# A routed expert kernel: the order of its 256-row and 384-row arms, and the place of one activation split at a phase's end

## The chip, the cores and the metric

The kernel runs on one core of one Trainium2 chip. The metric is the device time of one execution in microseconds (us). The kernel before took 606.57 us in the median of three runs (602.05 to 607.6).

## The reference

Two steps follow each other. A packed attention turns q, k, v and p into an activation x of 4608 rows by 512 columns; then each row goes through one of eight experts, the one that a small gate picks for it.

```python
def sm_attn(qq, kk, vv):
    a = softmax(scale * qq @ kk.T)
    return a @ vv
p_packed = sm_attn(p, k, v)                 # 8 x 8 heads, 576 rows, 32 packed rows
x = sm_attn(q, p_packed, p_packed)          # -> 4608 x 512
logits = x @ w_gate + modality_bias[modality_id]
e_idx = argmax(logits)                      # one of 8 experts for each row
for e in range(8):                          # w1: 512 x 1024, w2: 1024 x 512
    rows = e_idx == e
    out[rows] = gate_w[rows] * (relu(x[rows] @ w1[e]) @ w2[e])
```

## The kernel before

The attention fills about the first half of the time. The second half works through **slots**. A slot is a group of 256 or 384 rows of one expert, and which expert and how many rows is known only at run time: tables in SBUF (`tab_a`, `tab_b`, `tab_c`) hold for each slot its first row, its expert and flags. Column 3 of a table says whether the slot needs new weights, column 6 whether the slot has 384 rows, column 4 whether there is such a slot at all. Slots 0 and 1 belong to table a, slots 2 to 5 to table b, and slots 6 and up to table c; the first two groups always have 256 rows and overlap with the attention's end. Slots are written out one after another (`slot(n)`, called by `go_on(n)`); there is no hardware loop.

A slot n does the following.

- **Gather** (`fetch`, L761): GpSimd issues indirect transfers, one for each half row block, that bring the slot's rows of x into the tile `xt`. They can start when VectorE has read the rows of the slot before out of it.
- **Turn** (`turn`, L795): VectorE transposes the rows in 32x32 blocks, 16 instructions for each slot.
- **Split of x** (`st_xs`, L801 and L802): every operand is held as a high part and a low remainder. ScalarE casts the turned rows to the high part, VectorE subtracts to get the low part; both go to `x_hl` or, for slots of table c, `x_wide`. One pair of instructions for each 128 rows.
- **First product** (`st_1`, L818 in slots 0 to 5; `st_1_by_one`, L837 in later slots): TensorE makes 96 matmuls, three for each product of parts, into four PSUM banks. ScalarE evicts the high part with the Relu (L822, L841) and VectorE the low part (L824, L842).
- **Second product** (`st_2`, L873): 24 matmuls for each 128 rows into `ps_o`; ScalarE scales the result (L879), GpSimd scatters it to the output (L887).
- **New weights** (`sw`, L1048): under the flag of column 3 ScalarE and VectorE split W1 (L732, L736) or W2, and SyncE loads the next.

Each engine runs its own instruction stream in program order. A flag is read by the engine itself (`val`, L652 TENSOR_LOAD), then compared (COMPARE_AND_BRANCH). `tc.If(...)` with `.Else()` puts the first block straight behind the comparison; the block behind `Else` is reached by a jump, and the first block ends with a jump over it. Three helpers use that with column 6: `arms` for the first product (L1067 in the trace), `arms` for the rest of the second product, and `turn_of` for the turn (L1077). Outside of such blocks a scheduler places the instructions of each engine between the flags; `tc.issue_after(z)` holds an instruction behind z.

The place that the change touches beside the arms is **the phase's end**, slot 5, the last with table b: there `x_next(done)` splits the rows of slot 6 for `x_wide`, reads slot 6's flag of column 6 and splits its third 128 rows (L1097), and `sw(6, 0, ...)` reads slot 6's flag for W1 (L1048). `done` are the last two evictions of slot 5's first product. Even where the W1 flag is not set, TensorE's third matmul of slot 6 has to see VectorE past that block, since the block may write `w1l`. The turn of slot 7's rows stands in the same stretch.

Of the kernel before, what the change touches and what calls it, by code (L numbers as in the profile page):

```python
# [15 lines left out]
ET = mybir.EngineType  # L16
# [7 lines left out]
def packed_attn_moe_kernel(  # L24
# [114 lines left out]
    SA = [max(0, -((E * (P2 - 1) - m * 2 * S) // P2)) for m in NA]  # L139
# [55 lines left out]
    def feed(after=None):  # L195

        if not pending:
            return
        lists = {z[0][1] for z in pending if z[0][0] == "list"}
        n = next((n for n, z in enumerate(pending) if z[0][0] == "x" and not lists & set(range(need(z[0][1])))), 0)  # L200
        for ins in pending.pop(n)[1]():
            if after is not None:
                tc.add_manual_dep(ins, getattr(after, "ins", after).name, SYNC, reason="one by one")

    def flush(last=None):
        while any(last is None or z[0][0] == "x" and z[0][1] <= last for z in pending):
            feed()
# [220 lines left out]
    def ins_of(x):  # L428
        return getattr(x, "ins", x)
# [220 lines left out]
    def val(tb, s, col, engines, lo, hi):  # L650
        at = tb[0:1, s, col:col + 1] if len(tb.shape) == 3 else tb[s:s + 1, col:col + 1]
        return nc.values_load(at, engines=engines, min_val=lo, max_val=hi,  # L652
                              skip_runtime_bounds_check_because="bounded by the routing")
# [137 lines left out]
    def turn(ts):  # L791
        g, x = (xts[z][:, ts].rearrange("p t (j n) -> p (t j) n", n=P) for z in (1, 0))
        for z in range(0, P, Q):
            for w in range(0, P, Q):
                nc.vector.transpose(out=x[w:w + Q, :, z:z + Q], in_=g[z:z + Q, :, w:w + Q])  # L795

    def st_xs(M, ts):
        x = xts[0].rearrange("p t (j n) -> p j t n", n=P)
        hi, lo = (M["x"][:, :, z].rearrange("p j (t n) -> p j t n", n=P) for z in range(2))
        for t in ts:  # L800
            ia = nc.scalar.copy(out=hi[:, :, t], in_=x[:, :, t])  # L801
            iv = tt(out=lo[:, :, t], in0=x[:, :, t], in1=hi[:, :, t].bitcast(F32), op=ALU.subtract)  # L802
            if slow[0]:
                feed(ia)
        return ins_of(ia), ins_of(iv)
# [53 lines left out]
    def st_1_full(M):  # L859
        for f0 in range(0, KF, 2):  # L860
            all_of(st_1(M, f0, M["h", (f0 // 2) % M["nh"]]))
        return M["last"]

    def st_x_both(xt, M):
        for t in range(2):
            all_of(st_x(xt, M, t, W["t", t]))
        return M["ia"], M["iv"]
# [35 lines left out]
    def slot_of(n):  # L903
        ph = sum(n >= z for z in first[1:])
        return T[ph]["tab"], n - first[ph], ph

    def pre(n):
        if n < NS_:
            fetch(*slot_of(n), mts[n % 4], xts[n % 2 if n < 3 else 1], n)
# [113 lines left out]
    def sw(n, which, after=()):  # L1023
        if n >= NS_:
            return
        tb, s, ph = slot_of(n)

        def go():
            if n and which:
                k = 2 if n < SA[1] else 0  # L1030
                split_w(W, which, range(k))
                split_w(W, which, range(k, 4), eng=nc.gpsimd)
            elif n:
                split_w(W, which)
            nx = val(tb, s, 2, (ET.SP,), 0, E - 1)
            with tc.If(val(tb, s, 5, (ET.SP,), 0, 1) > 0):
                load_w(W, which, nx)

        if n == 0:
            go()  # L1040
        else:
            if s == 0:
                load_w(W, which, val(T[ph]["pre"], 0, 0, (ET.SP,), 0, E - 1))
            with ExitStack() as es:
                for z in after:
                    es.enter_context(tc.issue_after(z))
                flag = val(tb, s, 3, IFE + ((ET.Pool,) if which else ()), 0, 1)
            with tc.If(flag > 0):  # L1048
                go()
# [12 lines left out]
    def st_2_of(n, *ts):  # L1062
        for z, t in enumerate(ts):
            all_of(st_2(W, mts[n % 4], t, W["o", (z + (1 in ts)) % 2]))

    def arms(tb, s, engines, wide, full):
        with tc.If(val(tb, s, 6, engines, 0, 1) > 0) as three:  # L1067
            wide()
        with three.Else():
            full()  # L1070

    def turn_of(n):
        if n < SA[1]:
            turn(slice(0, 2))
        elif n < NS_:
            tb, s, _ = slot_of(n)
            with tc.If(val(tb, s, 6, (ET.DVE,), 0, 1) > 0) as wide:  # L1077
                turn(slice(0, 3))
            with wide.Else():
                turn(slice(0, 2))  # L1080

    def slot(n):
        tb, s, _ = slot_of(n)
        slow[0] = n < SA[1]
        X = W if n + 1 < SA[1] else V

        def x_next(done=()):
            if n + 1 >= NS_:
                return ()
            tn, sn, _ = slot_of(n + 1)  # L1090
            after = st_xs(X, (0, 1))
            if n + 1 >= SA[1]:
                with ExitStack() as es:
                    for z in done:
                        es.enter_context(tc.issue_after(ins_of(z)))
                    flag = val(tn, sn, 6, (ET.Activation, ET.DVE), 0, 1)
                with tc.If(flag > 0):  # L1097
                    st_xs(V, (2,))
            return after

        if n < SA[1]:
            done = st_1_full(W)
            if n == SA[0] - 1:
                st_2_of(n, 1)
                sw(n + 1, 0, st_x_both(xts[0], X))
            else:
                sw(n + 1, 0, x_next(done) + tuple(ins_of(z) for z in done))
            st_2_of(n, *((0,) if n == SA[0] - 1 else (1, 0)))
        else:
            if n == SA[1]:  # L1110
                x = W["x"].rearrange("p j z n -> p (j z n)")
                for z, nm in enumerate(("hh", "hl")):
                    k = (KF - HJ) * P3
                    W[nm] = [spare("rawk", n=HJ * P3).rearrange("p (j n) -> p j n", j=HJ),
                             x[:, z * k:z * k + k].rearrange("p (j n) -> p j n", j=KF - HJ)]
                W["x"] = V["x"]
            turn_of(n + 1)
            arms(tb, s, (ET.Activation, ET.PE, ET.DVE), lambda: st_1_by_one(W, P3), lambda: st_1_by_one(W, P2))
            x_next()
            sw(n + 1, 0)  # L1120
            pre(n + 2)
            flush()
            st_2_of(n, 1)
            arms(tb, s, (ET.Pool, ET.Activation, ET.PE), lambda: st_2_of(n, 2, 0), lambda: st_2_of(n, 0))
# [64 lines left out]
```

## Time and profile before

| | |
|---|---|
| median of three runs | 606.57 us |
| the profiled execution | 604.88 us, of which 603.2 us from the first to the last instruction |
| mean granted TensorE clock | 0.957 of full speed |
| TensorE busy | 560.6 us, 93% of the span |
| VectorE, ScalarE, GpSimd busy | 56%, 35%, 35% |

The trace holds slots 5 to 16 between 285 us and 597 us: slots 6, 9 and 14 have 384 rows, slots 7, 8, 10 to 13, 15 and 16 have 256. In rows of the trace PE is TensorE's matmul stream, PEld its weight loads, DVE VectorE, ACT ScalarE, POOL GpSimd; a trailing q marks the engine's sequencer.

### The profile page before, as it was taken

How to read it: one execution, taken by the hardware profiler on the slowest of the kernel's cores; microseconds unless marked ns; L12 is line 12 of the kernel's file. 1: busy time of each engine (PE TensorE's matmuls, PEld its weight loads, DVE VectorE, ACT ScalarE, POOL GpSimd, SP SyncE). 2: the span in 40 equal slices, each digit the busy share in tenths (PEclk: the TensorE clock that was granted, in tenths of full speed). 3: DMA queues.
4: the chain of work that ended last, by engine and by line, in shares of the span. 5: the costliest groups of instructions: out<-in, count | busy, mean ns of one | idle time of the engine just before them, and what ended most of it. 6: DMA issues, size and time to landing. Idle time of an engine off the chain costs nothing. (4 is left out here: it accounts for less than half of the span.)

```text
span 603.2 us, 12820 instructions
## 1 busy us (share of the span) xinstructions
PE 560.6 (93%) x4792; PEld 485.3 (80%) x4792; DVE 339.0 (56%) x785; ACT 213.0 (35%) x402; POOL 210.4 (35%) x259
## 2 busy tenths in 40 slices
PE   5998598977899999999979999999999999999995
PEld 4776475745697998998869898898989889998894
DVE  1499396829698716652842527656164374834540
ACT  2686585528342222211202222541222124521231
POOL 3002103742245364535321332256412513651331
PEclk9999799868699999999989999999999999999998
DMA  9799997828133951216441121364201201011331
GB/s 297 268 355 196 354 322 299 243 57 295 41 115 102 205 197 38 63 42 144 136 142 36 62 62 39 79 151 159 92 26 50 90 20 55 35 39 54 55 53 43
DMA packets 33704, 77.08 MB, mean 128 GB/s; under 512 B 7008, under 2 KB 7088, under 8 KB 32576
## 3 DMA queue, kind: packets, MB, share of 16 engines
q1 hardware_dynamic: 24224, 54.92, 29.6%
q0 software_dynamic: 8848, 20.75, 12.3%
q8 instruction: 52, 0.85, 0.7%
q14 instruction: 52, 0.43, 0.2%
q10 hardware_dynamic: 528, 0.13, 0.1%
HBM read 56.53 MB, written 19.26 MB: 126 GB/s over the span
## 5 line engine op out<-in xcount | busy, mean ns | idle before, releaser
L873 PE MATMUL ps_o<-rawq,rawk 128*128 128x512 f32 x460 | 147.2, 391 | 0.6 <-ACT rawk L822 0.6
L837 PE MATMUL ps_h<-x_wide,w1h 128*128 128x256 f32 (+1 forms) x704 | 143.4, 299 | 1.2 <-issue 1.1
L795 DVE STREAM_TRANSPOSE xt<-xt 32x256 f32<-32x256 f32 (+1 forms) x240 | 111.1, 463 | 29.7 <-DMA xt<-x_scr,mt 25.6
L837 PEld LDWEIGHTS ps_h<-x_wide,w1h 128*128 128x128 f32 x704 | 115.9, 190 | 2.7 <-issue 1.4
L761 POOL DMA_INDIRECT xt<-x_scr,mt x82 | 80.4, 980 | 93.8 <-DVE xt L795 37.3
L837 PE MATMUL ps_h<-x_wide,w1l 128*128 128x256 f32 (+1 forms) x352 | 106.3, 302 | 4.1 <-DVEq L1048 3.6
L873 PEld LDWEIGHTS ps_o<-rawq,rawk 128*128 128x128 f32 x460 | 86.1, 188 | 19.2 <-ACT rawk L822 0.8
L887 POOL DMA_INDIRECT out_dram<-ot,mt x37 | 38.4, 1038 | 128.9 <-ACT ot L879 100.2
L842 DVE SCALAR_TENSOR_TENSOR rawk<-ps_h,rawk 128x256 fp32r<-128x256 f32 (+1 forms) x66 | 29.5, 459 | 94.4 <-ACT rawk L841 66.2
L837 PEld LDWEIGHTS ps_h<-x_wide,w1l 128*128 128x128 f32 x352 | 66.9, 190 | 4.7 <-DVEq L1048 3.9
L879 ACT ACTIVATE ot<-ps_o,mt 128x512 f32<-128x512 f32 x35 | 24.1, 690 | 123.8 <-PE ps_o L873 77.8
L818 PE MATMUL ps_h<-x_hl,w1h 128*128 128x256 f32 x320 | 57.9, 283 | 0.5 <-ACTq L1048 0.4
L841 ACT ACTIVATE rawk<-ps_h 128x256 fp32r<-128x256 f32 (+1 forms) x66 | 26.3, 415 | 84.5 <-PE ps_h L837 69.5
L873 PE MATMUL ps_o<-qT,rawk 128*128 128x512 f32 x140 | 54.7, 391 | 0.0
L487 POOL DMA_INDIRECT lst<-meta,dsi x36 | 36.5, 1013 | 52.0 <-DVE nb L268 30.8
L818 PEld LDWEIGHTS ps_h<-x_hl,w1h 128*128 128x128 f32 x320 | 49.8, 189 | 0.8 <-ACTq L1048 0.5
L818 PE MATMUL ps_h<-x_hl,w1l 128*128 128x256 f32 x160 | 45.3, 284 | 0.0
L299 PE MATMUL ps<-rawv,a1T 64*64 64x128 f32 x576 | 31.0, 308 | 7.7 <-issue 6.2
L299 PEld LDWEIGHTS ps<-rawv,a1T 64*64 64x64 f32 x576 | 21.5, 151 | 17.0 <-issue 13.7
L873 PE MATMUL ps_o<-rawv,rawk 128*128 128x512 f32 x90 | 35.0, 389 | 0.0
L873 PE MATMUL ps_o<-rawq,x_hl 128*128 128x512 f32 x100 | 34.9, 390 | 0.0
L754 POOL DMA_DIRECT2D mt<-lst x19 | 14.8, 781 | 55.7 <-DMA out_dram<-ot,mt 25.1
(234 smaller groups left out, 827.4 us busy)
## 6 DMA issues: line engine op xcount, KB each, us to landing
rawq<-in_q_dram SPq DMA_DIRECT2D x8, 1152.0 KB
rawv<-in_v_dram SPq DMA_DIRECT2D x8, 1152.0 KB
x_scr<-xs SPq DMA_DIRECT2D x8, 1152.0 KB
raw<-in_moe_w_dram SPq DMA_DIRECT2D x32, 256.0 KB
rawk<-in_k_dram SPq DMA_DIRECT2D x7, 1152.0 KB
kT<-in_moe_w_dram SPq DMA_DIRECT2D x4, 1024.0 KB
qT<-in_moe_w_dram SPq DMA_DIRECT2D x3, 1024.0 KB
xt<-x_scr,mt POOLq DMA_INDIRECT x82
```

The lines of the kernel that those rows point to most:

```text
L299: nc.tensor.matmul(pp[u][os_, 0:P], a1T[rs, c, os_], v_t[rs, 2 * pr:2 * pr + 2, TOK[c], :], start=(c == 0), stop=(c == NC - 1), skip_group ...
L487: ins = ins_of(nc.gpsimd.indirect_dma_start(out=lst, out_offset=bass.IndirectOffsetOnAxis(ap=dsi[:, c:c + 1], axis=0), in_=meta[:, i * NC ...
L754: ins = free(nc.gpsimd.dma_start(mt[:, t:], lst[ds(off, rows), :].rearrange("(t p) w -> p t w", p=P)))
L761: return [free(nc.gpsimd.indirect_dma_start(out=xt[:, (t + 2) % 3, u * HW:u * HW + HW], out_offset=None, in_=x_scr[0:NA[ph] * 4 * S] if ph ...
L795: nc.vector.transpose(out=x[w:w + Q, :, z:z + Q], in_=g[z:z + Q, :, w:w + Q])
L818: nc.tensor.matmul(ps[:, f], M[a][:, j, (f0 + f) * P:(f0 + f) * P + P], M["x"][:, j, b, 0:P2], start=(n == 0), stop=(n == 3 * KD - 1))
L837: nc.tensor.matmul(ps, M[a][:, j, f * P:f * P + P], M["x"][:, j, b, cs], start=(n == 0), stop=(n == 3 * KD - 1))
L841: ia = nc.scalar.activation(out=hh, in_=ps, func=AF.Relu)
L842: iv = nc.vector.scalar_tensor_tensor(out=hl, in0=ps, scalar=0.0, in1=hh.bitcast(F32), op0=ALU.max, op1=ALU.subtract)
L873: nc.tensor.matmul(op, hid(M, a, j, 1, slice(t * P, t * P + P))[:, 0], M[b][j // 4][:, j % 4], start=(n == 0), stop=(n == 3 * KF - 1))
L879: ia = nc.scalar.activation(out=ot, in_=op, func=AF.Copy, scale=mt.bitcast(F32)[:, (t + 1) % 3, 2:3])
L887: nc.gpsimd.indirect_dma_start(out=out, out_offset=bass.IndirectOffsetOnAxis(ap=mt[:, (t + 1) % 3, 1:2], axis=0), in_=M["ot"][t == 0], in_ ...
```

## The change

In `arms` and `turn_of` the comparison is turned round, so that the 256-row block stands first and the 384-row block behind `Else`. In `slot`, `x_next` puts the split of x behind the instructions in `done`, together with the flag of column 6, where only that flag was held before; the flag for W1 is then held behind the split alone, whose instructions `x_next` returns.

```diff
     def arms(tb, s, engines, wide, full):
-        with tc.If(val(tb, s, 6, engines, 0, 1) > 0) as three:
+        with tc.If(val(tb, s, 6, engines, 0, 1) < 1) as two:
+            full()
+        with two.Else():
             wide()
-        with three.Else():
-            full()
...
-            with tc.If(val(tb, s, 6, (ET.DVE,), 0, 1) > 0) as wide:
+            with tc.If(val(tb, s, 6, (ET.DVE,), 0, 1) < 1) as two:
+                turn(slice(0, 2))
+            with two.Else():
                 turn(slice(0, 3))
-            with wide.Else():
-                turn(slice(0, 2))
...
             tn, sn, _ = slot_of(n + 1)
-            after = st_xs(X, (0, 1))
+            with ExitStack() as es:
+                for z in done:
+                    es.enter_context(tc.issue_after(ins_of(z)))
+                after = st_xs(X, (0, 1))
+                flag = n + 1 >= SA[1] and val(tn, sn, 6, (ET.Activation, ET.DVE), 0, 1)
             if n + 1 >= SA[1]:
-                with ExitStack() as es:
-                    for z in done:
-                        es.enter_context(tc.issue_after(ins_of(z)))
-                    flag = val(tn, sn, 6, (ET.Activation, ET.DVE), 0, 1)
                 with tc.If(flag > 0):
                     st_xs(V, (2,))
...
-                sw(n + 1, 0, x_next(done) + tuple(ins_of(z) for z in done))
+                sw(n + 1, 0, x_next(done))
```

ScalarE at the phase's end, before. L801 are the casts of slot 6's rows, L822 the evictions of slot 5's first product, L1048 the weight flags (`tab_b`: W2 of slot 5; `tab_c`: W1 of slot 6), L1077 its part in the turn's block.

```order
L801 CAST x_wide<-xt_141 128x4x128 x2
L652 TENSOR_LOAD tab_b
L1048 COMPARE_AND_BRANCH
...
L879 ACTIVATE ot_2875<-ps_o_2880,mt_136 128x512
L822 ACTIVATE rawk<-ps_h_2883 128x512
L822 ACTIVATE rawk<-ps_h_2884 128x512
L822 ACTIVATE rawk<-ps_h_2885 128x512
L822 ACTIVATE rawk<-ps_h_2886 128x512
L652 TENSOR_LOAD tab_c
L1097 COMPARE_AND_BRANCH
L801 CAST x_wide<-xt_141 128x4x128
```

ScalarE at the same place, with the change:

```order
L652 TENSOR_LOAD tab_b
L1048 COMPARE_AND_BRANCH
...
L879 ACTIVATE ot_2875<-ps_o_2880,mt_136 128x512
L822 ACTIVATE rawk<-ps_h_2883 128x512
L822 ACTIVATE rawk<-ps_h_2884 128x512
L822 ACTIVATE rawk<-ps_h_2885 128x512
L822 ACTIVATE rawk<-ps_h_2886 128x512
L801 CAST x_wide<-xt_141 128x4x128 x2
L652 TENSOR_LOAD tab_c
L1097 COMPARE_AND_BRANCH
L801 CAST x_wide<-xt_141 128x4x128
```

The two casts have moved from in front of the four evictions to behind them.

VectorE at the phase's end, before, from the third 128 rows of slot 6's x (L1097, behind slot 5's evictions) to the flag for W1 of slot 6 (L1048); the first two subtractions stand ahead of the evictions. L1077 is the turn of slot 7's rows with its two arms.

```order
L1097 COMPARE_AND_BRANCH
L802 TENSOR_TENSOR x_wide<-xt_141,x_wide 128x4x128
L1097 UNCONDITIONAL_BRANCH x2
L652 TENSOR_LOAD tab_c
L1077 COMPARE_AND_BRANCH
L795 STREAM_TRANSPOSE xt_141<-xt_142 32x12x32 x16
L1077 UNCONDITIONAL_BRANCH
L795 STREAM_TRANSPOSE xt_141<-xt_142 32x8x32 x16
L1077 UNCONDITIONAL_BRANCH
L652 TENSOR_LOAD tab_c
L1048 COMPARE_AND_BRANCH
L736 TENSOR_TENSOR w1l<-raw_118,w1h 128x4x256 x4
```

VectorE at the same place, with the change:

```order
L1097 COMPARE_AND_BRANCH
L802 TENSOR_TENSOR x_wide<-xt_141,x_wide 128x4x128
L1097 UNCONDITIONAL_BRANCH x2
L802 TENSOR_TENSOR x_wide<-xt_141,x_wide 128x4x128 x2
L652 TENSOR_LOAD tab_c
L1048 COMPARE_AND_BRANCH
L736 TENSOR_TENSOR w1l<-raw_118,w1h 128x4x256 x4
L1036 UNCONDITIONAL_BRANCH
L1048 UNCONDITIONAL_BRANCH
L652 TENSOR_LOAD tab_c
L1077 COMPARE_AND_BRANCH
L795 STREAM_TRANSPOSE xt_141<-xt_142 32x8x32 x16
```

The flag for W1 now stands in front of slot 7's turn instead of behind it, the first two subtractions of x (L802 x2) stand behind the evictions and the third, and the turn's arm with 8 blocks in a row (256 rows) comes first.

GpSimd at the same place, as a difference (minus: before; plus: with the change). L754 reads slot 8's list of rows, L761 gathers slot 8's rows, L887 scatters an output block of slot 5.

```order
 L754 DMA mt_136<-lst 128x3x4
 L1097 UNCONDITIONAL_BRANCH
-L1077 UNCONDITIONAL_BRANCH
-L1048 UNCONDITIONAL_BRANCH
+L1048 UNCONDITIONAL_BRANCH
+L1077 UNCONDITIONAL_BRANCH
+L887 DMA out_dram<-ot,mt_137 4608x512
...
 L761 DMA xt_142<-x_scr,mt_136 128x256 x4
-L887 DMA out_dram<-ot,mt_137 4608x512
```

One scatter has moved ahead of slot 8's gather; in later slots the two arms change places on each engine and the order within them is unchanged.

## Rows read from the trace of the kernel before

**Rows 1.** Busy time on the page: us, share of the span, instructions.

```profile
PE 560.6 (93%) x4792; PEld 485.3 (80%) x4792; DVE 339.0 (56%) x785; ACT 213.0 (35%) x402; POOL 210.4 (35%) x259
```

**Rows 2.** TensorE's waits from 285 us on: us in total, times, longest.

```profile
PE ps_h L837 <- DVEq L1048: 3.6, 1, 3.6
PE ps_h L837 <- issue: 1.5, 3, 0.7
PE ps_o L873 <- ACT rawk L822: 0.6, 1, 0.6
```

**Rows 3.** First products, slots 5 to 10 and 12: stretch, length, PE busy (matmuls), clock, DMA.

```profile
285.28:297.58 12.30, 11.69 (x97) 1.00 0.46 117
308.88:331.12 22.24, 18.63 (x97) 0.92 0.12 37
347.49:359.96 12.47, 11.96 (x98) 1.00 0.26 74
370.86:382.39 11.53, 11.53 (x97) 1.00 0.23 70
393.32:410.22 16.90, 16.90 (x97) 1.00 0.55 124
426.56:438.82 12.26, 11.90 (x97) 1.00 0.29 90
...
472.18:485.04 12.86, 12.08 (x98) 1.00 0.28 84
```

**Rows 4.** The same view, second products of slots 4 and 5.

```profile
274.35:285.28 10.93, 10.93 (x51) 1.00 0.75 172
297.58:308.88 11.30, 11.30 (x49) 1.00 0.72 246
```

**Rows 5.** Timeline of TensorE: start, us, instruction, idle before it and its releaser.

```profile
297.58 0.51 PE L873 MATMUL ps_o<-rawq,rawk 128*128 128x512 f32 x1 [0.62 <-ACT rawk L822]
...
308.88 0.52 PE L837 MATMUL ps_h<-x_wide,w1h 128*128 128x384 f32 x2
313.01 0.69 PE L837 MATMUL ps_h<-x_wide,w1l 128*128 128x384 f32 x1 [3.61 <-DVEq L1048]
```

**Rows 6.** Busy time in one stretch: length, PE, PEld, DVE, ACT, POOL, clock.

```profile
310.00:315.00 5.00, 1.99 (x6) 1.99 (x7) 2.82 (x7) 0.00 (x0) 1.52 (x2) 0.79 0.04 9
```

**Rows 7.** Timeline of VectorE, 285 us to 343 us.

```profile
285.61 9.31 DVE L795 STREAM_TRANSPOSE xt<-xt 32x384 f32<-32x384 f32 x16 [8.54 <-DMA xt<-x_scr,mt]
...
297.56 2.48 DVE L824 SCALAR_TENSOR_TENSOR rawk<-ps_h,rawk 128x512 fp32r<-128x512 f32 x4 [0.60 <-ACT rawk L822]
299.97 0.68 DVE L802 TENSOR_TENSOR x_wide<-xt,x_wide 128x512 fp32r<-128x512 f32 x1
305.72 7.18 DVE L795 STREAM_TRANSPOSE xt<-xt 32x256 f32<-32x256 f32 x16 [5.07 <-DMA xt<-x_scr,mt]
317.11 0.56 DVE L842 SCALAR_TENSOR_TENSOR rawk<-ps_h,rawk 128x384 fp32r<-128x384 f32 x1 [4.21 <-issue]
...
335.32 7.19 DVE L795 STREAM_TRANSPOSE xt<-xt 32x256 f32<-32x256 f32 x16 [0.29 <-DVE x_wide L802]
```

**Rows 8.** Timeline of ScalarE at the phase's end.

```profile
295.02 1.14 ACT L801 CAST x_wide<-xt 128x512 fp32r<-128x512 f32 x2 [12.76 <-DVE xt L795]
...
296.95 2.05 ACT L822 ACTIVATE rawk<-ps_h 128x512 fp32r<-128x512 f32 x4
```

**Rows 9.** Timeline of GpSimd: the first gather for slot 8.

```profile
313.17 0.99 POOL L761 DMA_INDIRECT xt<-x_scr,mt  x1 [4.99 <-DVEq L1048]
```

**Rows 10.** Timeline of GpSimd in slot 7: last gather transfer for slot 9.

```profile
350.89 0.94 POOL L761 DMA_INDIRECT xt<-x_scr,mt  x1 [0.30 <-issue]
```

**Rows 11.** Timeline of ScalarE in slot 7: its first four evictions.

```profile
351.07 0.39 ACT L841 ACTIVATE rawk<-ps_h 128x256 fp32r<-128x256 f32 x1 [2.69 <-issue]
354.66 0.94 ACT L841 ACTIVATE rawk<-ps_h 128x256 fp32r<-128x256 f32 x3 [3.21 <-PE ps_h L837]
```

**Rows 12.** Queues on the page: packets, MB, share of 16 engines' span.

```profile
q8 instruction: 52, 0.85, 0.7%
```

## The prediction

> **What bounds the kernel now.** The page's first part says that TensorE is busy for 560.6 us, 93% of the span [rows 1], so only time in which TensorE waits, or runs slowly, can be won. The change leaves the program alone up to slot 5, so I read the waits of TensorE from 285 us on: there are only three kinds, 3.6 us once for VectorE's sequencer at L1048, 0.6 us once for ScalarE's evictions, and 1.5 us in three pieces with no releaser ("issue") [rows 2]. The view by stretches places them. A first product of 256 rows takes 11.53 us when nothing is in its way, one of 384 rows 16.90 us; slots 5, 6, 7, 10 and 12 take longer, slot 6 by far, with 22.24 us [rows 3]. The timeline shows slot 6 start at 308.88, stop after two matmuls, and go on at 313.01 [rows 5]. In the stretch from 310 to 315 us the mean granted clock is 0.79, that is a part at the lower of its two levels (1.2 instead of 2.4 GHz), behind that idle time [rows 6].
>
> VectorE's timeline says why slot 6 stops: VectorE stands in its queue at the turn of slot 7's rows, waits 5.07 us for their transfer and turns them from 305.72 to 312.90 [rows 7]. W1's flag for slot 6 comes behind that in its program, and TensorE's third matmul wants to see VectorE past the flag. The flag itself is not set in this execution: no L736 stands between the rows at 299.97 and 317.11 [rows 7].
>
> **The change at the phase's end.** Three things move.
>
> First, ScalarE's casts of x. Before, they wait 12.76 us for the turn of slot 6's rows and so hold the evictions of slot 5's first product, which run as four in a row from 296.95 to 299.00, after the product has ended [rows 8]. Slot 5's stretch, first product to start of the second, is 12.30 us instead of 11.53, 0.77 too much [rows 3], and its second product, still chasing evictions, is 11.30 instead of the 10.93 of slot 4, 0.37 too much [rows 4]. With the evictions in front, the first three are done on ScalarE long before; VectorE finishes its turn at 285.61 + 9.31 = 294.92 and then evicts three times 0.62 (2.48 / 4), until 296.8; the product ends at 285.28 + 11.53 = 296.81. The fourth pair is over by about 298.1 and is wanted only in the last quarter of the second product. I take both: -0.77 - 0.37 = -1.14.
>
> Second, the flag ahead of slot 7's turn. Slot 6's first product should then take what slot 9's, also of 384 rows, takes: 16.90 instead of 22.24 [rows 3], that is -5.34. Of this 3.61 us is the wait [rows 5]; the rest, about 1.7, is matmuls at the lower clock, and it goes with the idle time that stands before it.
>
> Third, the split itself now ends later; the work that hides it is slot 5's second product, 10.93 us. ScalarE: fourth eviction over at about 297.5, two casts 1.14 [rows 8], the flag's read, for which I allow 0.6, the third cast half of 1.14: 299.8. VectorE: three parts of 0.68 [rows 7]: 301.9, then the flag for W1, again 0.6: 302.5. TensorE wants all that at 308.88 - 1.14 = 307.74. It is 5.2 us early. If this cover were gone, the wait would come back one for one.
>
> What is late next? Slot 7's turn cannot start before its rows land at 305.72, nor end before 312.90, as before. Behind it in VectorE's queue stand slot 6's own evictions. The first bank is full at 307.74 + 16.90 / 8 = 309.9 and wanted again, as four banks go round, at 307.74 + 4 x 2.11 = 316.2; VectorE is free 3.3 us before that, for two flags and an eviction of 0.56 [rows 7]. It just holds, and costs nothing; a miss would cost at most that eviction and flags again, about 1 us. Slot 8's gather still starts behind that turn at 313.17 [rows 9]; four transfers at some 1.25 us apart end about 322, an estimate from rows 9 and 10 (0.94 to 0.99 us for one, 0.30 between); slot 8's turn, which before began at 335.32 behind VectorE's own split and no transfer [rows 7], moves to 328.8. Covered by 6 us. The scatter that passes slot 8's gather on GpSimd is one transfer of about 1 us while that gather waits 4.99 us anyway [rows 9]: nothing. SyncE's loads wait for flags that come no later: nothing. From slot 7 on everything moves forward together.
>
> **The change to the arms.** No work is added or taken: 22 decisions on each of TensorE and ScalarE (two in each of 11 slots, 6 to 16), fewer on the others. Each decision has one far jump, either in front of its arm or behind it; the swap changes which slots have it in front. Before, the 256-row slots jump in front: slot 8 does so and takes 11.53 us with TensorE busy for 11.53. The 384-row slots jump behind: slot 9 takes 16.90 with 16.90 busy [rows 3]. So both kinds cost nothing on TensorE where nothing else is going on. Slots 7, 10 and 12 lose 0.94, 0.73 and 1.33 us, 3.0 in sum [rows 3]. In slot 7 ScalarE's second eviction comes at 354.66, 3.2 us after the one before [rows 11], just as the gather for slot 9 is landing, whose last transfer GpSimd issued at 350.89 [rows 10]; a slot that jumps just the same, slot 8, has no such loss. I read these as the gather's doing, not the jump's. Bounds: -3.0 if all three are jumps, and on the other side the loss per jump of the rival below. I take 0.
>
> The Trainium skill ("Runtime: NRT & Kernel Launch", Instruction fetch mechanics) says that a taken branch whose target is outside the loaded window makes the engine fetch code before it goes on, and that straight code is fetched ahead. The trace's instruction queue moved 52 packets in 0.7% of 16 engines' 603.2 us, so 1.3 us each [rows 12]; paid on the path by 16 jumps that would be 21 us, and slots 8 and 9 show none of it. By that rule the jumps would be worth something; by the rows they are worth nothing.
>
> **Sum.** -0.77 - 0.37 - 5.34 + 0 = -6.48 us, against the profiled execution's 604.88 us (span 603.2, 1.7 around it): 598.4. That execution lies 1.7 us under the median of 606.57 and 2.8 over the lowest run; profiled and timed runs together have a mean of 605.3, and 605.3 - 6.48 gives 598.8. I say 599.
>
> **Rivals.**
> - *The front jumps are what slots 7, 10 and 12 lose.* Then the arms give 3.0 more: 604.88 - 9.48 = 595.4. For it: all three are jumped to, and ScalarE's first eviction in slot 7 is late too, with no releaser [rows 11]. Against: slot 8 and four more 256-row slots like it (11, 13, 15, 16, each 11.5) jump and lose nothing [rows 3].
> - *Slower: the jump behind the 256-row arm is dear.* A 256-row product runs through its 96 matmuls in 11.53 us instead of 16.90, so the engine's sequencer has less time in hand for the jump that now follows. Its place is the end of both arms in eight slots, 16 jumps. At 1.0 us each (the mean of the three losses above) that is +16.0 - 6.48: 614.4. It undoes the gain from 0.4 us a jump, and is over 1% slower from (6.48 + 6.05) / 16 = 0.78. Against: the jump behind the 384-row arm costs nothing.
> - *Slot 6 waits all the same.* VectorE is late with the split or the flag, since it now takes the third part first and waits for ScalarE there. Only the first term stays: 604.88 - 1.14 = 603.7. It needs 5.2 us of delay.
>
> **How the numbers follow.** Forecast 0.70, first rival 0.15, second 0.05, third 0.10. The timed runs before spread over 5.5 us, which I put around each: the forecast's own range is 595.6 to 601.1 (lowest and highest run less 6.48). For 8 in 10 I take in most of the first rival and the third, cutting at the ends: 594 to 604. A measurement of this kernel can tell about 1% (6.05 us) from no change. The forecast is only 0.4 us beyond that, so it counts 0.58 as faster and the rest as the same; the first rival 0.9 faster; the third 0.1; the second mostly slower: faster 0.55, same 0.40, slower 0.05.
>
> **What would show it.** Right: in slot 5 no wait of TensorE for L822; slot 6's first product near 16.9 us with no wait for L1048 and full clock; W1's flag before slot 7's turn on VectorE, that turn still at about 305.7; slots 9 and 14 at 16.90 and the clean 256-row slots at 11.53 with arms swapped. Slots 7, 10 and 12 at 11.53 throughout would speak for the first rival. Gaps of TensorE between first and second product in 256-row slots would speak for the second. A new wait in slot 6 for L802 or L842, or a later landing of slot 7's rows, would break the largest term.

## The result, and the profile after

The changed kernel takes 598.54 us in the median of 21 runs (593.07 to 601.71); the kernel before took 605.39 us in 21 runs beside it (599.37 to 607.91). The ratio is 0.9886, with a 95% interval from 0.9858 to 0.9913. Forecast were 599 us, within 594 to 604.

TensorE's waits from 285 us on, in the view of waits (engine, what waits, what released it: us in total, times, longest):

```profile
PE ps_h L837 <- issue: 1.4, 3, 0.7
```

Two of the three kinds in [rows 2] are gone, the wait for the flag at L1048 and the one for L822. The view by stretches (length, then PE, PEld, DVE, ACT, POOL busy, clock, DMA share, GB/s) of slot 5's two products, slot 6's first product, and the first products of slots 7 to 10 and 12:

```profile
287.12:298.64 11.52, 11.52 (x97) 11.52 (x96) 10.52 (x19) 2.49 (x4) 0.97 (x1) 1.00 0.50 121
298.64:309.57 10.93, 10.93 (x51) 9.01 (x49) 5.39 (x11) 2.83 (x5) 5.58 (x6) 1.00 0.72 264
309.57:326.47 16.90, 16.90 (x97) 16.90 (x96) 8.47 (x18) 3.45 (x7) 4.40 (x5) 1.00 0.16 48
342.81:355.18 12.37, 11.95 (x97) 11.58 (x96) 2.69 (x7) 3.17 (x8) 5.25 (x6) 1.00 0.26 76
366.10:377.62 11.52, 11.52 (x97) 11.52 (x96) 5.28 (x12) 3.39 (x8) 5.58 (x6) 1.00 0.23 71
388.55:405.45 16.90, 16.90 (x97) 16.90 (x96) 8.69 (x19) 7.81 (x12) 10.66 (x10) 1.00 0.55 127
421.79:434.05 12.26, 11.91 (x98) 11.60 (x96) 2.69 (x7) 3.13 (x8) 5.68 (x6) 1.00 0.28 89
467.41:480.30 12.89, 12.18 (x98) 11.77 (x97) 2.87 (x8) 3.16 (x8) 7.54 (x8) 1.00 0.29 85
```

Against [rows 3] and [rows 4], slot 5's first product is 0.78 us shorter, its second 0.37, and slot 6's first product 5.34, now at full clock throughout. Slots 7, 10 and 12 lose about what they lost before (0.84, 0.73 and 1.36 us over 11.53; before: 0.94, 0.73 and 1.33). ScalarE and VectorE at the phase's end, in the timeline (start, us, instruction, idle before it and its releaser), to be held against [rows 8] and [rows 7]:

```profile
290.20 0.60 ACT L822 ACTIVATE rawk<-ps_h 128x512 fp32r<-128x512 f32 x1 [2.15 <-PE ps_h L818]
...
298.84 0.60 ACT L822 ACTIVATE rawk<-ps_h 128x512 fp32r<-128x512 f32 x1 [2.28 <-PE ps_h L818]
299.34 1.65 ACT L801 CAST x_wide<-xt 128x512 fp32r<-128x512 f32 x3
```

```profile
301.02 1.90 DVE L802 TENSOR_TENSOR x_wide<-xt,x_wide 128x512 fp32r<-128x512 f32 x3 [0.85 <-ACTq L1048]
307.19 7.18 DVE L795 STREAM_TRANSPOSE xt<-xt 32x256 f32<-32x256 f32 x16 [4.27 <-DMA xt<-x_scr,mt]
314.40 1.02 DVE L842 SCALAR_TENSOR_TENSOR rawk<-ps_h,rawk 128x384 fp32r<-128x384 f32 x2
...
330.64 7.18 DVE L795 STREAM_TRANSPOSE xt<-xt 32x256 f32<-32x256 f32 x16 [0.19 <-DVE x_wide L802]
```

The evictions follow TensorE one by one and the casts stand behind the last. VectorE is through with the split at 302.92, 6.6 us before slot 6 begins at 309.57. Slot 7's turn still waits for its rows.

The two profiled executions tell less than the timed runs. From the start of slot 5 to the end of the last matmul, 311.42 us became 304.86, that is -6.56. But this execution began slot 5 at 287.12 instead of 285.28, in code that the change leaves alone (+1.84), and from the last matmul to the end of the span took 7.95 us instead of 6.49 (+1.46), so that the span fell by only 3.3 us, from 603.2 to 599.9. In the experiments I therefore give three numbers: the ratio of timed runs, the **middle** (slot 5's start to the end of the last matmul) and the **tail** (from there to the end of the span).

### The profile page after: what moved, and what is told of

Same layout as the page of the kernel before. It is cut to its first block, busy times and chain, and to the rows that moved or that the text cites. A ratio compares the mean times of both kernels' runs of the same rounds, so it can differ in the third digit from the quotient of the medians.

```text
span 599.9 us, 12863 instructions
## 1 busy us (share of the span) xinstructions
PE 558.3 (93%) x4792; PEld 485.4 (81%) x4792; DVE 339.8 (57%) x785; ACT 213.6 (36%) x402; POOL 211.0 (35%) x259
## 5 line engine op out<-in xcount | busy, mean ns | idle before, releaser
L873 PE MATMUL ps_o<-rawq,rawk 128*128 128x512 f32 x460 | 146.8, 390 | 0.0
L761 POOL DMA_INDIRECT xt<-x_scr,mt x82 | 80.6, 983 | 98.5 <-DVE xt L795 30.8
L873 PEld LDWEIGHTS ps_o<-rawq,rawk 128*128 128x128 f32 x460 | 86.3, 188 | 17.6
L887 POOL DMA_INDIRECT out_dram<-ot,mt x37 | 38.6, 1043 | 122.9 <-ACT ot L879 91.3
L873 PE MATMUL ps_o<-qT,rawk 128*128 128x512 f32 x140 | 54.7, 391 | 0.0
L299 PE MATMUL ps<-rawv,a1T 64*64 64x128 f32 x576 | 28.4, 308 | 8.8 <-issue 7.1
L873 PE MATMUL ps_o<-rawv,rawk 128*128 128x512 f32 x90 | 35.0, 389 | 0.0
L873 PE MATMUL ps_o<-rawq,x_hl 128*128 128x512 f32 x100 | 34.9, 390 | 0.0
L754 POOL DMA_DIRECT2D mt<-lst x19 | 14.9, 782 | 52.3 <-DMA out_dram<-ot,mt 23.8
```

Of the source, the lines that this page charges most:

```text
L299: nc.tensor.matmul(pp[u][os_, 0:P], a1T[rs, c, os_], v_t[rs, 2 * pr:2 * pr + 2, TOK[c], :], start=(c == 0), stop=(c == NC - 1), skip_group ...
L754: ins = free(nc.gpsimd.dma_start(mt[:, t:], lst[ds(off, rows), :].rearrange("(t p) w -> p t w", p=P)))
L761: return [free(nc.gpsimd.indirect_dma_start(out=xt[:, (t + 2) % 3, u * HW:u * HW + HW], out_offset=None, in_=x_scr[0:NA[ph] * 4 * S] if ph ...
L873: nc.tensor.matmul(op, hid(M, a, j, 1, slice(t * P, t * P + P))[:, 0], M[b][j // 4][:, j % 4], start=(n == 0), stop=(n == 3 * KF - 1))
L887: nc.gpsimd.indirect_dma_start(out=out, out_offset=bass.IndirectOffsetOnAxis(ap=mt[:, (t + 1) % 3, 1:2], axis=0), in_=M["ot"][t == 0], in_ ...
```

## The experiments

The experiments ran on four chips, and these are of two sorts: on the chip of e1 to e4 the kernel before took 603.7 us, on that of f1 to f3 605.2, but on that of e5 to e7 only 584.1, and on that of e8 and e9 584.3 and 582.5. The two profiles of before and after are of the sort of 604. Kernels of one sort are compared in what follows; only e5 is set against [rows 3], for slot 6, whose product of 384 rows takes 16.90 us on both.

| kernel | ratio | 95% interval | middle | tail |
|---|---|---|---|---|
| before (profile shown ahead) | | | 311.42 | 6.49 |
| after | 0.9886 | 0.9858 to 0.9913 | 304.86 | 7.95 |
| e1_phase_only | 0.9877 | 0.9840 to 0.9914 | 304.74 | 7.94 |
| e2_arms_only | 0.9995 | 0.9969 to 1.0021 | 312.90 | 6.85 |
| e3_split_only | 1.0015 | 0.9992 to 1.0038 | 312.59 | 7.06 |
| e4_flag_try | 0.9883 | 0.9849 to 0.9917 | 306.27 | 6.38 |
| f1_after | 0.9907 | 0.9875 to 0.9939 | 305.06 | 8.02 |
| f2_no_gather | one run | | 301.95 | 10.50 |
| f3_two_gathers | one run | | 301.96 | 12.77 |
| e5_busy_gap (chips of 584 us) | one run | | 309.15 | 7.68 |
| e6_no_gather (584 us) | one run | | 301.95 | 10.52 |
| e7_end_first (584 us) | 0.9928 | 0.9903 to 0.9954 | 301.95 | 8.38 |
| e8_spread, e9_spread_again (584 us) | 0.9893, 0.9883 | 0.9855 to 0.9930, 0.9849 to 0.9918 | 301.95 | 6.74, 7.11 |

### The two parts of the change, each alone

**e1_phase_only** is the kernel before with the new `x_next` and `sw(n + 1, 0, x_next(done))`, the arms as before. **e2_arms_only** is the kernel before with the three decisions of `arms` and `turn_of` swapped.

> The part at the phase's end alone, with the arms as in the kernel before. If the phase's end is the whole gain (the forecast's theory): ratio to the kernel before 0.989 (-6.5 us of 605), slot 5's start to the last matmul about 304.9 us long where the kernel before shows 311.4 and the changed one 304.9, slot 6's first product 16.9 to 17.1 us at full clock, and slots 7, 10 and 12 still 0.7 to 1.4 us over 11.69. If the arms had a share in the gain (first rival, at most 3.0 us): ratio 0.994 and those three slots still lose, while in the changed kernel they would not. If the arms' new order is also what made the tail longer (the last matmul to the end of the span is 6.49 us before, 7.93 after), the tail here is back at 6.5; if not, anything between 6.5 and 8.

> The arms swapped alone, the phase's end as before. Forecast's theory (jumps of either kind are free): ratio 1.000, between 0.997 and 1.003, first products of 256 rows 11.5 to 11.7 us where no gather disturbs them, of 384 rows 16.9 to 17.1, slot 6 with its wait of 3.6 us for the flag at L1048 as before. First rival (front jumps cost the three slots 3.0 us): 0.995. Second rival (the jump behind the 256-row arm is dear, from 0.4 us each at 16 places): 1.011 or more, with gaps of TensorE between the first and the second product. If the swap lengthens the tail by itself: 1.002 and a tail near 7.9 us instead of 6.5.

e1, by stretches: slot 5's two products and slot 6's first.

```profile
282.88:294.41 11.53, 11.53 (x98) 11.53 (x96) 10.35 (x19) 2.48 (x4) 0.97 (x1) 1.00 0.52 122
294.41:305.33 10.92, 10.92 (x50) 9.01 (x49) 5.10 (x11) 2.83 (x5) 5.07 (x6) 1.00 0.77 266
305.33:322.24 16.91, 16.91 (x98) 16.91 (x97) 8.94 (x19) 3.44 (x7) 4.72 (x5) 1.00 0.16 48
```

e2, the same view: first products of slots 6, 8 and 9.

```profile
308.83:332.17 23.34, 19.49 (x97) 19.17 (x96) 8.03 (x17) 3.44 (x7) 4.86 (x5) 0.85 0.12 35
...
372.10:383.63 11.53, 11.53 (x97) 11.53 (x96) 5.28 (x12) 3.38 (x8) 5.60 (x6) 1.00 0.23 71
394.56:411.46 16.90, 16.90 (x98) 16.90 (x96) 8.68 (x19) 7.80 (x12) 10.66 (x10) 1.00 0.54 124
```

The phase's end is the whole gain: e1's middle is the changed kernel's to 0.12 us, and its ratio is as low. The arms are worth nothing either way. With the swap, slots 8 and 9 take what they took without it, and slots 7, 10 and 12 lose 1.13, 0.78 and 1.10 us where before they lost 0.94, 0.73 and 1.33. e2's middle is 1.48 us longer than that of before, and 1.10 of it is slot 6, whose stretch had more of the lower clock this time (0.85 instead of 0.92); the timed runs show nothing of it.

### The two steps at the phase's end, each alone

**e3_split_only** puts the split behind the evictions but leaves the flag for W1 behind slot 7's turn. **e4_flag_try** moves the flag and leaves the split.

```diff
         ia = nc.scalar.activation(out=ot, in_=op, func=AF.Copy, scale=mt.bitcast(F32)[:, (t + 1) % 3, 2:3])
+        M["st2", t] = ins_of(ia)
...
-                sw(n + 1, 0, x_next(done) + tuple(ins_of(z) for z in done))
+                after = x_next(done)
+                if n < SA[1] - 1:
+                    sw(n + 1, 0, after)
             st_2_of(n, *((0,) if n == SA[0] - 1 else (1, 0)))
+            if n == SA[1] - 1:
+                sw(n + 1, 0, (W["st2", 1],))
```

This is e3, with `x_next` as in the changed kernel; and e4, with `x_next` as before:

```diff
-                sw(n + 1, 0, x_next(done) + tuple(ins_of(z) for z in done))
+                sw(n + 1, 0, x_next(done))
```

> The split of x behind the evictions, but the flag for W1 left behind slot 7's turn on VectorE, the arms as before. Forecast's terms: -0.77 - 0.37 = -1.14 us, ratio 0.998; TensorE's wait for L873's operands in slot 5 is gone, slot 6's first product still stops about 4 us for L1048 and takes 22 us or a little more, since the product starts 1.1 us earlier and the turn does not end earlier: then the wait grows by what was won, 3.6 + 1.1 = 4.7 us, and the ratio is 1.000. Which of the two it is says whether the first term is worth anything without the second. Rival (the evictions' order is what holds slot 6): 0.990.

> The flag for W1 ahead of slot 7's turn alone: it no longer waits for slot 5's last evictions, the split of x stays ahead of those evictions, the arms as before. Forecast's terms: -5.34 us, ratio 0.991, slot 6's first product near 17 us without a wait for L1048, while slot 5 still takes 12.3 us with a wait of 0.6 us of TensorE for L822. If the split's place matters for the flag too: slot 6 waits still, ratio 0.998 to 1.000.

e3: waits of TensorE, then the stretches of slot 5's products and slot 6's first (in e3 lines behind 880 are one higher).

```profile
PE ps_h L837 <- DVEq L1049: 4.6, 1, 4.6
...
PE ps_o L873 <- ACTq L1049: 1.2, 1, 1.2
```

```profile
287.05:298.58 11.53, 11.53 (x97) 11.53 (x96) 10.09 (x18) 2.49 (x4) 0.85 (x1) 1.00 0.48 116
298.58:309.50 10.92, 10.92 (x50) 9.01 (x49) 5.54 (x11) 2.83 (x5) 4.79 (x6) 1.00 0.78 267
309.50:334.03 24.53, 18.74 (x98) 18.08 (x96) 9.31 (x20) 4.52 (x9) 4.88 (x5) 0.93 0.11 33
```

e4: stretches of slot 5's products and slot 6's first.

```profile
284.48:296.98 12.50, 11.69 (x98) 11.48 (x96) 10.43 (x19) 2.37 (x5) 2.08 (x2) 1.00 0.50 120
296.98:308.26 11.28, 11.28 (x48) 9.03 (x49) 6.05 (x12) 2.72 (x5) 4.07 (x5) 1.00 0.73 247
308.26:325.17 16.91, 16.91 (x98) 16.91 (x97) 7.98 (x17) 3.45 (x7) 4.87 (x5) 1.00 0.17 48
```

e4 shows the flag alone: slot 6 takes 16.91 us, and the middle is 5.15 us shorter than before, close to the 5.34 of the sum; slot 5 keeps both its losses. Its middle is 1.53 us longer than e1's, but its tail is 1.56 us shorter: from slot 5's start to the end of the span the two take the same, 312.65 and 312.68 us (before: 317.91), and their timed ratios agree too (0.9883 and 0.9877). So in these two executions the flag alone gives all of the gain that reaches the end of the program; that the split's part reaches it is not shown.

e3 shows that the split's 1.15 us are won in slot 5, both terms as forecast, and lost again in slot 6: TensorE comes earlier to a flag that does not come earlier, and waits 4.6 us instead of 3.6. So the first term has its worth from the second; alone it is nothing. Another 1.2 us of e3's stretch come from the edit itself: in it ScalarE reads slot 6's flag for W2 behind slot 6's last eviction, where before it stood ahead of the first, and TensorE waits for that at the second product (the row for L873).

### What the rest of slot 6's loss was

**e5_busy_gap** is the kernel before with 16 matmuls of 128x512 into `ps_t`, which nothing reads, behind slot 5's second product.

```diff
+            if n == SA[1] - 1:
+                for z in range(16):
+                    nc.tensor.matmul(W["t", z % 2].rearrange("p j n -> p (j n)"), W["2h"][0][:, 0, 0:P],
+                                     W["2h"][0][:, 0], start=True, stop=True)
```

> The kernel before, with 16 matmuls of 128 x 512 (about 0.23 us each at full clock, 3.7 us in all, into a PSUM bank that nothing reads) added behind slot 5's second product, so that TensorE works through most of the wait for the flag at L1048. Slot 5's second product with them, and slot 6's first product, lie together between the same two points, so read the time from slot 6's first matmul's place in the flow to the product's end: before, slot 5's second product begins at 297.58 and slot 6's first product ends at 331.28 (33.70 us). If the 1.7 us beyond the wait are the lower clock that follows the idle time (forecast): the granted clock stays at full level, the flag is passed at the same point, and that time falls by 1.5 to 1.8 us, to about 32.0. If the 1.7 us are something else (the banks, the evictions, code): it stays at 33.7, at full clock all the same. If the gap is too short to matter for the clock once the wait is filled but the added work ends after the flag, up to 0.5 us are lost.

Stretches of slot 5's second product with the added work, and of slot 6's first; then TensorE's timeline behind the flag and at the end of that stretch.

```profile
274.79:289.70 14.91, 14.90 (x64) 12.04 (x65) 9.27 (x20) 2.62 (x5) 3.92 (x5) 1.00 0.57 187
289.70:308.61 18.91, 17.35 (x97) 16.69 (x95) 5.24 (x10) 4.52 (x9) 4.86 (x5) 1.00 0.14 43
```

```profile
290.60 0.45 PE L837 MATMUL ps_h<-x_wide,w1l 128*128 128x384 f32 x1 [0.37 <-DVEq L1048]
...
291.24 0.34 PE L837 MATMUL ps_h<-x_wide,w1l 128*128 128x384 f32 x1
...
307.08 0.34 PE L837 MATMUL ps_h<-x_wide,w1l 128*128 128x384 f32 x1
308.62 0.50 PE L873 MATMUL ps_o<-rawq,rawk 128*128 128x512 f32 x1 [1.21 <-ACTq L1048]
```

In the kernel before, the second matmul on `w1l` behind the flag and the last of the product (the first stands in [rows 5]):

```profile
314.14 0.52 PE L837 MATMUL ps_h<-x_wide,w1l 128*128 128x384 f32 x1
...
330.95 0.33 PE L837 MATMUL ps_h<-x_wide,w1l 128*128 128x384 f32 x1
```

With TensorE kept at work, the granted clock stays at its full level through slot 6 (1.00 instead of 0.92). The flag is passed about where it was, 15.81 us after the second product's start (before: 15.43), but from there to the end of the product's last matmul it takes 16.82 us (290.60 to 307.42) instead of 18.27 (313.01 to 331.28): 1.45 us less. Undisturbed it takes 16.70 (slot 9 of the kernel before, from 393.68). So slot 6's 5.34 us come apart without a rest. Its third matmul started 3.77 us late, which is the wait of 3.61 and 0.16 in which two matmuls would have overlapped. The clock took 1.45, and 0.12 is left, which e5 has too, behind its own short pause: the first matmul there took 0.45 us instead of 0.34.

From the second product's start to the end of slot 6's first product, as the expectation counts it, 33.70 us became 32.63 (274.79 to 307.42): 1.07 less, not 1.5 to 1.8, as the flag is passed 0.38 later. Slot 6's second product starts no earlier for that (33.82 us after 274.79, before 33.54), since this edit, like e3, put ScalarE's flag for W2 behind the evictions, which cost 1.21.

### Slots 7, 10 and 12

**e6_no_gather** and **f2_no_gather** are one kernel, the changed one with `if n < 9` before the gathers of x; **f3_two_gathers** issues two for each slot from 9 on, instead of four or six; **f1_after** is the changed kernel on the chip of f2 and f3.

> The changed kernel without the gathers of x for slots 9 and up (those slots work on rows that were gathered before, so the output's values differ; all other work is there, the scatters too). If the losses of slots 7, 10 and 12 are the gather's doing (forecast): their first products take 11.53 us from start to start of the second, as the others do, instead of 12.37, 12.26 and 12.88, ScalarE's evictions there follow TensorE within 0.2 us, and the time from slot 5's start to the last matmul is 304.86 - 2.9 = 302.0 us or less. If the losses are code loading or anything else that does not hang on the gather: 12.3 to 12.9 as before, and 304.9.

> The changed kernel once more, on the chip of the two kernels below. On chips on which slots 7, 10 and 12 lose time (as in the first runs): slot 5's start to the last matmul 304.9 us, those three first products 12.3 to 12.9 us. On a chip like that of the last three runs, on which no kernel lost anything in them: 301.95 us, all 11.53, and the ratio to the kernel before still 0.989 +- 0.003, since the wait for the flag was there too.

> The same kernel as e6_no_gather (the changed kernel without the gathers of x for slots 9 and up, whose values are then wrong), beside the changed kernel on one chip. If the changed kernel loses time in slots 7, 10 and 12 there: the gather theory says 11.53 us for all three here, ScalarE's evictions within 0.2 us of TensorE, 301.95 us from slot 5's start to the last matmul; a cause without the gather says 12.3 to 12.9 us again. If the changed kernel loses nothing there, nothing is told apart.

> The changed kernel with two of the four or six gathers for each of the slots 9 and up (half the columns of x; values wrong for the rest). If the evictions come late only as long as gathers are under way: two gathers take some 2.5 us to issue instead of 5 or 7.5, the latest eviction is late by about 1 to 2 us instead of 4.5, four PSUM banks of 1.44 us each hide that, and the three slots take 11.53 us. If a single gather is enough to hold them up: the latest eviction is still over 4 us late and 0.7 us or more is lost in each. On a chip without these losses: 11.53 us, nothing told apart.

On the chip of e5 to e7 there was nothing to test: e7, with all gathers, takes 11.53 us in all three slots. Its stretches there:

```profile
321.46:332.99 11.53, 11.53 (x97) 11.53 (x96) 2.97 (x7) 3.38 (x8) 5.22 (x6) 1.00 0.28 82
399.61:411.14 11.53, 11.53 (x98) 11.53 (x97) 2.97 (x7) 3.38 (x8) 5.67 (x6) 1.00 0.30 96
444.51:456.04 11.53, 11.53 (x97) 11.52 (x96) 3.12 (x8) 3.38 (x8) 7.25 (x8) 1.00 0.31 95
```

The chip of f1 to f3 shows the losses. f1, the same three slots, and ScalarE's first evictions in slot 7:

```profile
341.62:354.12 12.50, 11.97 (x97) 11.61 (x96) 2.79 (x7) 3.17 (x8) 5.23 (x6) 1.00 0.25 75
420.71:432.95 12.24, 11.91 (x97) 11.61 (x96) 2.70 (x7) 3.16 (x8) 5.68 (x6) 1.00 0.28 90
466.31:479.32 13.01, 12.08 (x97) 11.74 (x96) 2.94 (x8) 3.17 (x8) 7.55 (x8) 1.00 0.29 84
```

```profile
344.52 0.39 ACT L841 ACTIVATE rawk<-ps_h 128x256 fp32r<-128x256 f32 x1 [2.02 <-PE ps_h L837]
348.80 0.94 ACT L841 ACTIVATE rawk<-ps_h 128x256 fp32r<-128x256 f32 x3 [3.89 <-PE ps_h L837]
```

f2, without gathers (lines one higher), and f3, with two: slot 7's first product, and ScalarE's first two evictions in f2.

```profile
343.10:354.63 11.53, 11.53 (x98) 11.53 (x97) 2.97 (x7) 3.38 (x8) 1.77 (x2) 1.00 0.08 25
```

```profile
344.74 0.38 ACT L842 ACTIVATE rawk<-ps_h 128x256 fp32r<-128x256 f32 x1 [0.76 <-PE ps_h L838]
346.18 0.38 ACT L842 ACTIVATE rawk<-ps_h 128x256 fp32r<-128x256 f32 x1 [1.06 <-PE ps_h L838]
```

```profile
340.14:351.67 11.53, 11.53 (x97) 11.52 (x96) 2.97 (x7) 3.38 (x8) 1.80 (x2) 1.00 0.12 36
```

Without the gathers no slot loses anything and the middle falls by 3.1 us, from 305.06 to 301.95. In f1 ScalarE's second eviction of slot 7 starts 4.1 us after TensorE has filled the bank, in f2 0.04. So on this chip the gathers are needed for the loss, and two of them do not make it: f3's latest eviction in the three slots is 0.16 us late, where 1 to 2 us were expected. On the other sort of chip six gathers in the same places do not either, at the same rate of issue. Why is open. Code loading is no candidate in slot 7: in f1 no packet of an instruction queue moves between 331 and 351 us, and the late evictions start between 344.52 and 349.34. f2 and f3 are not faster as a whole, as their tails are 2.5 and 4.8 us longer: GpSimd's drain behind its last scatter (L1184 in f1) takes 5.13 and 6.77 us there and 2.75 in f1, for a reason that no run shows.

**e8_spread** and **e9_spread_again** are one kernel that asks whether it is the row of transfers without a pause: the changed kernel with a pause of some 3 us on GpSimd behind each pair (four subtractions on 128x288 numbers that are no longer used).

```diff
+        def gap():
...
+                for z in range(4):
+                    ins = nc.gpsimd.tensor_tensor(out=l, in0=l, in1=l, op=ALU.subtract)
```

> The changed kernel with GpSimd's gathers for slots 9 and up issued in pairs: after each two it does four dummy subtractions on 128 x 288 (about 0.7 us each by the rows of that shape, some 3 us with a flag) before the next two; all gathers are there. If a row of four to seven transfers is what makes the evictions late (two made none late): slots 7, 10 and 12 take 11.53 us, the latest eviction is under 1 us late there, the time from slot 5's start to the last matmul is 301.95 us instead of 304.9, the ratio to the kernel before 0.984 instead of 0.989. If the number of gathers in a slot counts and not how close they stand: the evictions are as late, only spread, and 304.9 stays. If the last gather now comes too late for the turn (it ends about 6 us later than before): a wait of VectorE for it and up to 1 us lost in the slot after a 384-row gather.

> The kernel of e8_spread once more. On the chip of its first run no slot lost anything, so the pairs were not put to the test there. On a chip on which the changed kernel loses about 3 us in slots 7, 10 and 12: if a row of four to seven transfers is what makes the evictions late, those slots take 11.53 us, the time from slot 5's start to the last matmul is 301.95 us instead of 304.9 and the ratio 0.984; if the number in a slot counts and not how close they stand, 304.9 and 0.989. On a chip without those losses: 301.95 and 0.989 again, and the question stays open.

Both ran on a chip of 584 us, and on chips of that sort no kernel lost anything in these slots. The pauses cost nothing there, as slot 7 of e8 shows, with GpSimd busy for 9.73 us instead of 5.22:

```profile
321.25:332.78 11.53, 11.53 (x97) 11.52 (x96) 2.97 (x7) 3.38 (x8) 9.73 (x14) 1.00 0.22 70
```

Whether they win the 3 us where these are lost was not seen. e8 and e9 have the same ratio as the changed kernel, 0.989 and 0.988, on a chip where its middle should be 301.95 too, as it was without losses in e7; they are no better version by what was measured.

### The tail

**e7_end_first** is the changed kernel with the decision in `run` turned round.

```diff
-            with tc.If(val(tb, s, 4, ALLE, 0, 1) > 0) as more:
-                go_on(n)
-            with more.Else():
-                last_out(n - 1)
+            with tc.If(val(tb, s, 4, ALLE, 0, 1) < 1) as end:
+                last_out(n - 1)
+            with end.Else():
+                go_on(n)
```

> The changed kernel with the last decision turned round: where there is no further slot, the last scatter stands straight behind the comparison and the next slot is jumped to, before it was the other way. If GpSimd's 4.4 us from the comparison at L1150 to the scatter's code (589.32 to 593.76) is a jump over the code of slots 17 to 24: the last scatter is issued about 1.0 us after the last matmul instead of 3.2, the tail is 5.8 us instead of 7.9, and the ratio to the kernel before is 0.985 (the changed one's 0.989 less 0.0035), if the short jumps that each slot now takes are free. If these cost anything on the path: 0.1 us in each of 11 slots eats half of the gain (0.987), 0.2 us all of it. If the tail's 4.4 us is not the jump: no change, 0.989, tail 7.9.

The last scatter on GpSimd in the kernel before (the last matmul ends at 596.70) and in f1 (590.98), where it is jumped to, and in e7, where it is not (567.72):

```profile
598.35 1.00 POOL L887 DMA_INDIRECT out_dram<-ot,mt  x1 [5.02 <-POOLq L1150]
```

```profile
594.29 1.00 POOL L887 DMA_INDIRECT out_dram<-ot,mt  x1 [6.67 <-ACTq L1150]
```

```profile
568.86 1.00 POOL L887 DMA_INDIRECT out_dram<-ot,mt  x1 [4.50 <-POOLq L1150]
```

The scatter does come 1.14 us after the last matmul instead of 3.31. But the end does not: the jump over the unused slots' code now stands behind the scatter, where GpSimd's next instruction comes 3.2 us after the comparison at L1150 (569.79 to 572.98), and the tail is 8.38 us. The distance was moved, not removed. The short jumps cost nothing (the stretches of e7 above). With the tail no shorter, e7's ratio of 0.9928 is no gain; that it lies above 0.989 I put down to the tail, about 1.4 us longer than that of e8 and e9; but these ran on another chip, so that is not shown.

The Trainium skill ("Runtime: NRT & Kernel Launch", Instruction fetch mechanics) says that a taken branch to a target outside the loaded pages waits for a fetch. The 3.2 us here, and 4.6 in f1 between GpSimd's comparison at 588.29 and the scatter's first instruction at 592.87, agree with that, as does the nothing of the arms' jumps, which leap over some 200 instructions at most, if their targets were loaded already; no run shows where the border is.

## Why the prediction was right

**The sum.** The three terms were -0.77, -0.37 and -5.34. They came out as -0.78, -0.37 and -5.34, and all else between slot 5 and the last matmul as -0.07, together -6.56 against -6.48. What the sum did not hold is the tail, 1.46 us longer in the profiled execution, so that from slot 5's start to the end of the span the two profiles show 5.10 us won. Timed, 605.39 less 598.54 is 6.85, within 5.3 to 8.6 by the interval; the same kernel in f1 gave 5.96 (605.17 less 599.21). That 598.54 lies so near to 599 is therefore in part luck: the base of 605.3 was a mean of four executions that spread over 5.5 us, and a term of some 1.5 us may be missing. The interval also lies clear of 1 at a width of 0.0055, so the 1% that the prediction took as the least that can be told from no change was too coarse.

**The tail.** It is 7.7 to 8.0 us in the changed kernel, f1, e1 and e5, and 6.4 to 7.1 in before, e2, e3, e4, e8 and e9. It goes with one piece of GpSimd's time, from the comparison at L1150 to the scatter's first instruction: 4.1 to 4.6 us in the first four, 2.8 to 3.5 in the others. The place of the split and the flag does not decide it, since e5 has both where they were before, and e8 and e9 have both where the changed kernel has them. The cause stays open.

**The flag.** Right, with the mechanism shown from both sides: e4 moves the flag alone and wins 5.15, e3 leaves it and wins nothing. That the rest beyond the wait is clock was right for 1.45 of 1.7 us (e5); the other 0.3 belong to the pause itself, as e5 shows above.

**The first two terms.** Right in size up to the last matmul; whether they shorten the whole is not shown (e4 against e1). The prediction set them beside the third as if they stood by themselves, and priced its third rival by them ("Only the first term stays", 603.7 us). e3 is near to that case: slot 6 waits all the same, and the 1.14 us come back as a longer wait. The rival's time should have been that of no change. It did not come to pass; only its chance of 0.10 and the upper end of the range, 604, hung on that price.

**The cover.** The split ends on VectorE 15.8 us after slot 5's start (302.92 less 287.12), where 17.2 with the flag's read was worked out, and slot 7's turn runs from 20.1 to 27.2, where it ran from 20.4 to 27.6. Slot 6's first eviction on VectorE starts at 314.40, behind the turn and 2.5 us after TensorE has filled the bank, and ends 3.1 us before the bank is wanted again (309.57 + 4 x 2.11 = 318.0): "it just holds" was right, and VectorE was free 3.6 us before the bank was wanted (at 314.37), where 3.3 were worked out. Slot 8's turn starts 43.52 us after slot 5's start, forecast were 328.8 less 285.28, that is 43.52 too.

**The arms.** Right: nothing (e2). Both rivals that gave the jumps a price, of -3.0 and of +16 us, are out.

**Slots 7, 10 and 12.** "The gather's doing, not the jump's" is right as far as it goes (f2). It was said from one slot of one trace, where slot 8, with four gathers in a row, loses nothing, though its evictions come late too (up to 1.48 us there, 2.61 in f1). Slots 11, 13, 15 and 16, which the prediction names and its rows do not show, do take 11.53 us each. What it takes beside the gathers, a chip of the one sort and more than two of them, was not foreseen, and f3 and the chips of 584 us show it.

## What to carry to other kernels

When an engine waits for a flag, look at what stands ahead of the flag in the reader's queue, and move the flag rather than speed up its surroundings: here one flag past one turn was worth 5.2 us, of which about a quarter was not the wait but the clock behind it. A gain in front of a wait that does not move is given back in full, so terms along one path must be summed in order, from the last wait to the first. And where an edit adds instructions near a flag, see where the scheduler puts the next flag: twice here it slid behind the evictions and cost 1.2 us.

## What the runs showed that was not expected

- The same program takes 582 to 584 us on some chips and 604 to 605 on others. In the profiles the difference lies ahead of slot 5: it begins at 262.5 to 266.7 us on the former, at 282.9 to 287.4 on the latter. From slot 5 on the two sorts differ only by the 3 us of slots 7, 10 and 12.
- On the chips of 604 us, ScalarE's evictions come up to 4.65 us after TensorE has filled the bank while four or more gathers are issued in a row (f1, slot 12); with two gathers in a row they come 0.16 us late at most in slots 7, 10 and 12, and 0.41 in slot 11 (f3). Four PSUM banks of 1.44 us hide most of it, so that a slot loses 0.7 to 1.5 us.
- The order of two arms behind a flag, up to some 200 instructions each on TensorE, is free at 22 decisions (ratio 0.9995); one jump over the code of unused slots at the program's end takes GpSimd 2.6 us (f3) to 4.6 us (f1).
